# Work of an attention and feed-forward kernel moved from VectorE and ScalarE to GpSimd, with fewer warm-up products in front

## The chip, the cores and the metric

The kernel runs on one core of a Trainium2 chip. The metric is the device time of one execution in microseconds (us), as the median of several runs. The profile is one further execution, taken by the hardware profiler.

## What is computed

Banded attention with a few global keys, then two feed-forward layers on its output. Cut to what matters:

```python
scores = q @ k.T / 8                      # 2 batches, 8 heads, 768 positions, 64 wide
bias = -slopes * dist                     # dist: distance of query and key
scores = where(is_global | is_local, scores + bias, -1e9)
a = exp(scores - max(scores))
a = a / (sum(a) + 1e-9)
x = (a @ v)                               # 1536 tokens x 512
h = maximum(x @ w_in, 0); x = (h * h) @ w_out            # 512 -> 2048 -> 512
h = x @ w2_in; g = where(h >= 1, h, where(h <= -1, 0, (h + 1) ** 2 / 4)); out = g @ w2_out
```

A query keeps the keys of the last n_local = 96 positions and the first n_global = 8; both numbers are inputs, 64-bit integers in memory. The weights of the first layer's two matrices and of the second's come as 64-bit floating point; everything is computed in 32-bit precision, the feed-forward products as three products of parts (high and low) of 32-bit operands.

## The kernel before

**Attention.** There are 12 blocks of 128 queries, and each is done in two halves of four heads, 24 halves. A half (`probabilities`, `turned`, `result`) multiplies q by k for two rings of keys (L868), adds the mask and takes the negated row minimum in one DVE operation (L890), takes exponentials with their sum on ACT (L895), adds 1e-9 to the four sums (L900, DVE), takes reciprocals (L902, DVE), scales the four heads' probabilities (`Plan.scale`: L153 on ACT, L155 on DVE, L157 on POOL), turns them on PE (L918), copies them back (L129 on ACT, L130 on DVE) and multiplies them by v (L954). With a block's second half the result leaves as high and low parts (L129, L140) into `x`, from which the layers multiply. Three buffers `pr` and `mn` hold the probabilities and the small numbers of three halves.

**Weights.** `float32` loads a chunk of 128x1024 numbers in two halves of 512 columns as pairs of 32-bit words (tile `raw`, two buffers) and makes 32-bit numbers of them (tile `whole`). In 64 half chunks altogether ACT scales the upper word, read as a float, by 2 to the power -112 (L153); DVE shifts that left by 3 (L470), puts in the lower word's three upper bits (L473) and the sign of the upper word (L477). `parts` then splits them into a high and a low part in a `slot` (L129 on ACT, L140 on DVE). The chunks of the second layer are prepared ahead, with sums of their quarters that POOL or DVE subtracts (L503), and kept in device memory.

**The layers.** `Ffn.h` multiplies x by a chunk's first part (L535), ACT and DVE take the square of the positive part (L550, L552; later L555), `halves` splits it (L129, L140), `Ffn.y` multiplies by the second part (L733). The second layer runs in pairs (L652, L702). The first 19 events of the layers are interleaved with the attention's halves.

**What sets the order.** Nothing is placed by hand: every operation is given to `Plan` with its engines, an estimated duration, a due time and what it reads and writes; `Plan.emit` walks through an estimated time and gives each engine the operation that is due first among those that could start, and issues all in the order of the starts so found. Where an operation has several engines, another engine takes it if it would be done there sooner. Operations marked `port` use what POOL and DVE share: the planner starts such an operation only when the last one has ended, and lets DVE take another one in between (`PASS`). Where PE has nothing for longer than `FGAP`, the planner puts in filling products of 256 columns on a tile of zeros, `warm`: L1342 into bank 7 while the first four halves run, L1344 into bank 0 after that. Eight products of 512 columns on the same tile (`WARM`, L1339) begin the program; the product L1169 spreads `n_local` and `n_global` over the partitions, and the masks are made from its result (L1004 and on).

## Time and profile before

| | us |
|---|---|
| three runs | 613.58 to 614.92, median 614.76 |
| the profiled execution | 613.96 |
| its span, first to last instruction | 612.2 |
| PE busy (matmul) | 599.7 |
| PE loading weights (PEld) | 514.0 |
| DVE busy | 481.0 |
| ACT busy | 351.5 |
| POOL busy | 58.1 |

The span is one core's. PE's ends are modelled, so a busy PE is not a PE at its peak, and PE is busy with warm-up and filling products as well. A share of the whole span is a mean over stages with different limits: up to about 165 us attention and the first layer run side by side, up to about 302 us the weights of both layers are made, and then the second layer runs on what was kept. Lines such as L470 are lines of the kernel before; one line can stand for several engines' or tiles' operations, where a helper issues them. Idle time in front of an instruction is put down to whatever ended last; on an engine that is not the bound it costs nothing.

### The profile page before, as it was taken

To read this page: it belongs to the slowest core of one execution; us is meant where nothing else is said; L and a number is where in the kernel's file an instruction comes from. 1 tells how busy PE (TensorE), PEld (TensorE's weight loads), DVE (VectorE), ACT (ScalarE), POOL (GpSimd) and SP (SyncE) were. 2 spreads that over 40 slices of the span, in tenths; PEclk is the share of its full clock that TensorE was granted. 3 is DMA by queue.
4 is the path that set the end of the run, shared out by engine and by line. 5 is a ranking of instruction groups with operands and counts; after the bars stand their busy time and mean duration, and the time that the engine had idled before them with its cause. 6 is when DMAs were issued, how large, how long until landed. Compare 5 with 4: busy or idle time off the path is not lost. (4 is left out here: it accounts for less than half of the span.)

```text
span 612.2 us, 9673 instructions
## 1 busy us (share of the span) xinstructions
PE 599.7 (98%) x3438; PEld 514.0 (84%) x3438; DVE 481.0 (79%) x1031; ACT 351.5 (57%) x731; POOL 58.1 (9%) x88
## 2 busy tenths in 40 slices
PE   8999999999999999999999999999999999999995
PEld 5778987878888888888888898888899999888884
DVE  7999999965638988898566389999897788887862
ACT  7898877765547766674447464545553444444331
POOL 4120111010001104233200000000000000000000
PEclk9999999999999999999999999999999999999999
DMA  8553544430114879988512202323220022223002
GB/s 303 166 185 118 186 147 154 150 121 22 38 36 124 272 235 304 359 321 283 193 68 70 94 27 69 118 73 107 82 96 1 35 104 96 96 94 96 26 2 108
DMA packets 25790, 79.24 MB, mean 129 GB/s; under 512 B 2948, under 2 KB 2948, under 8 KB 25732
## 3 DMA queue, kind: packets, MB, share of 16 engines
q1 hardware_dynamic: 25730, 78.52, 38.0%
q8 instruction: 29, 0.48, 0.3%
q14 instruction: 29, 0.24, 0.1%
q10 hardware_dynamic: 2, 0.00, 0.0%
HBM read 62.78 MB, written 15.73 MB: 128 GB/s over the span
## 5 line engine op out<-in xcount | busy, mean ns | idle before, releaser
L658 DVE TENSOR_TENSOR pr<-bank,pr 128x384 f32<-128x384 f32 x112 | 60.2, 554 | 23.4 <-PE bank L652 22.5
L140 DVE TENSOR_TENSOR g<-r,g 128x512 fp32r<-128x512 f32 (+2 forms) x74 | 48.9, 660 | 34.7 <-ACT g L129 33.8
L550 ACT ACTIVATE r<-bank 128x512 f32<-128x512 f32 (+1 forms) x52 | 29.2, 562 | 59.7 <-PE bank L535 58.9
L129 ACT ACTIVATE g<-r 128x512 fp32r<-128x512 f32 (+2 forms) x74 | 42.7, 577 | 24.9 <-DVE r L567 14.2
L895 ACT ACTIVATE pr<-pr,mn 128x256 f32<-128x256 f32 (+1 forms) x96 | 45.9, 480 | 4.6 <-DVE mn L890 4.2
L563 ACT ACTIVATE r<-pr,small 128x384 f32<-128x384 f32 x43 | 26.2, 615 | 32.8 <-DVE pr L658 32.7
L153 ACT ACTIVATE whole<-raw 128x512 f32<-128x512 f32 x52 | 33.9, 668 | 9.1 <-DMA raw<-in_moe_w_out_dram 3.2
L477 DVE SCALAR_TENSOR_TENSOR whole<-raw,whole 128x512 uint32<-128x512 uint32 x52 | 36.7, 712 | 0.4
L890 DVE CUSTOM_DVE_ANT_0 pr<-bank,m 128x256 f32<-128x256 f32 (+1 forms) x96 | 33.4, 397 | 4.2 <-PE bank L954 4.1
L473 DVE SCALAR_TENSOR_TENSOR whole<-raw,whole 128x512 uint32<-128x512 uint32 x52 | 35.9, 702 | 0.3
L157 POOL TENSOR_SCALAR pr<-pr,mn 128x256 f32<-128x256 f32 (+1 forms) x38 | 21.4, 570 | 120.3 <-DVE mn L902 57.9
L868 PEld LDWEIGHTS bank<-nat,nat 64*128 64x128 f32 x352 | 22.7, 190 | 7.6 <-issue 2.7
L565 DVE SCALAR_TENSOR_TENSOR r<-r 128x384 f32<-128x384 f32 x43 | 23.8, 556 | 5.9 <-ACT r L563 5.1
L868 PE MATMUL bank<-nat,nat 64*128 64x128 f32 x352 | 27.0, 288 | 1.3 <-DVE mn L890 1.2
L563 ACT ACTIVATE nat<-pr,small 128x384 f32<-128x384 f32 x21 | 12.9, 617 | 24.5 <-DVE pr L658 24.5
L470 DVE TENSOR_SCALAR whole<-whole 128x512 uint32<-128x512 uint32 x52 | 22.9, 448 | 4.0 <-ACT whole L153 3.7
L129 ACT ACTIVATE pr<-bank 128x512 f32<-128x512 f32 (+2 forms) x46 | 23.5, 521 | 3.4 <-PE bank L652 2.1
L567 DVE TENSOR_TENSOR r<-pr,r 128x384 f32<-128x384 f32 x43 | 23.8, 557 | 1.2
L954 PE MATMUL bank<-pr,nat 128*64 128x128 f32 x352 | 24.0, 277 | 0.6 <-DVE mn L890 0.3
L918 PE MATMUL bank<-ident,pr 128*128 128x128 f32 x176 | 23.9, 275 | 0.0
L954 PEld LDWEIGHTS bank<-pr,nat 128*64 128x64 f32 x352 | 19.7, 136 | 4.8 <-issue 2.0
L918 PEld LDWEIGHTS bank<-ident,pr 128*128 128x128 f32 x176 | 20.0, 140 | 2.8 <-issue 0.5
(347 smaller groups left out, 1753.6 us busy)
## 6 DMA issues: line engine op xcount, KB each, us to landing
raw<-in_moe_w_in_dram SPq DMA_DIRECT2D x32, 512.0 KB, 4.4
raw<-in_moe_w_out_dram SPq DMA_DIRECT2D x32, 512.0 KB, 4.8
whole<-sums SPq DMA_DIRECT2D x14, 512.0 KB, 3.3
kept<-whole SPq DMA_DIRECT2D x12, 512.0 KB, 6.3
whole<-kept SPq DMA_DIRECT2D x12, 512.0 KB, 3.3
whole<-kept SPq DMA_DIRECT2D x13, 384.0 KB, 3.1
sums<-pr SPq DMA_DIRECT2D x8, 512.0 KB, 5.8
nat<-in_k_dram SPq DMA_DIRECT2D x12, 256.0 KB, 3.7
```

What stands on the lines that cost most here:

```text
L129: ("act", ns_act(n) - 30 * psum, lambda: nc.scalar.activation(out=at(out), in_=in_, func=ACTF.Copy), False),
L140: ways = [("dve", ns_dve(n), lambda: nc.vector.tensor_tensor(out=at(out), in0=in_, in1=at(hi).bitcast(F32), op=ALU.subtract), not psum)]
L153: ("act", ns_act(n) + (0 if isinstance(by, float) else 107), lambda: nc.scalar.activation(out=out, in_=in_, func=ACTF.Copy, scale=by), False),
L473: op("dve", ns_dve(512), d + 0.2, lambda h=h: nc.vector.scalar_tensor_tensor(out=word[:, h], in0=low[:, h], scalar=29, in1=word[:, h], op0 ...
L477: op("dve", ns_dve(512), d + 0.3, lambda h=h: nc.vector.scalar_tensor_tensor(out=word[:, h], in0=high[:, h], scalar=0x80000000, in1=word[: ...
L563: op("act", ns_act(N) + 64, due, lambda: nc.scalar.activation(out=r, in_=h, func=ACTF.Relu, bias=self.half, scale=0.5), keys, [kr])
L658: op("dve", ns_dve(W), start + step[name] + 0.2 - G_LEAD, lambda: nc.vector.tensor_tensor(out=to, in0=area[kb], in1=in1, op=ALU.add), [("b ...
L868: nc.tensor.matmul(**c)
L890: op("dve", ns_dve(w), due, lambda e=e: nc.vector.tensor_tensor_reduce(out=pr[:, e, :w], in0=self.banks[kbs[e % 2]][:, e // 2 * 256:e // 2 ...
L895: op("act", ns_act(w) + 200, due, lambda e=e: nc.scalar.activation(out=pr[:, e, :w], in_=pr[:, e, :w], func=ACTF.Exp, bias=mn[:, e:e + 1], ...
L918: self.nc.tensor.transpose(self.banks[kbs[m]][:, o:o + P], pr[:, 2 * m + e, c * P:(c + 1) * P], self.ident)
L954: nc.tensor.matmul(**c)
```

## The change

Five parts. The weights' signs: GpSimd multiplies the upper words, read as floats, by 0.0 in place, which leaves a zero with the sign; DVE then needs two operations in place of three (lower word shifted right, or the sign; number shifted left by 3, or that). The scaling of probabilities goes to GpSimd alone from the third block on (`SCALE`; the first two blocks keep DVE and GpSimd). The 1e-9 is added on GpSimd. The warm-up products are five and two in place of eight, the two with a due time among the first scores. The first two blocks' v is due later, behind their k and q. In the planner, POOL and DVE no longer wait for each other: a POOL operation is reckoned 1.3 times as long, and a DVE operation that meets one up to 90 ns longer; `BEGIN` and the lags of the two numbers' loads have other values.

```diff
-WARM, LAG = 8, 950
+AGAIN = 2
+WARM, LAG = 5, 950
...
-PASS = 1.0
+SHARE, GIVE = 1.3, 90
...
-SCALE, SCALE0 = ("act", "dve", "pool"), ("dve", "pool")
-CONV = ("act",)
+SCALE, SCALE0 = ("pool",), ("dve", "pool")
+CONV, SIGN = ("act",), ("pool",)
...
-    BEGIN = {"act": 2000, "dma": 1680, "words": 1680, "pool": 1080, "dve": 630, "pe": 1120}
+    BEGIN = {"act": 2560, "dma": 1360, "words": 740, "pool": 1260, "dve": 980, "pe": 1390}
...
-            if port > t and engine == "dve" and ops[i][0]["dve"][2]:
...
-                    others = max(free[e], t, port if ways[e][2] else 0)
-                    own = max(t, port if ways[engine][2] else 0)
+                    others, own = max(free[e], t), t
...
             if ways[engine][2]:
-                t = max(t, port)
-                port = t + ns
+                if engine == "pool":
+                    ns *= SHARE
+                    port = t + ns
+                elif engine == "dve" and port > t:
+                    ns += min(GIVE, port - t)
...
             self.plan.scale(512, d, f32[:, h], high[:, h].bitcast(F32), 2.0 ** -112, [(*kr, n)], [(*kc, n)], engines=CONV)
-            op("dve", ns_dve(256), d + 0.1, lambda h=h: nc.vector.tensor_scalar(
-                out=word[:, h], in0=word[:, h], scalar1=3, scalar2=None, op0=ALU.logical_shift_left,
-            ), (), [(*kc, n)], port=True)
+            self.plan.scale(512, d, high[:, h].bitcast(F32), high[:, h].bitcast(F32), 0.0, [(*kc, n)], [(*kr, n)], engines=SIGN)
             op("dve", ns_dve(512), d + 0.2, lambda h=h: nc.vector.scalar_tensor_tensor(
-                out=word[:, h], in0=low[:, h], scalar=29, in1=word[:, h],
+                out=low[:, h], in0=low[:, h], scalar=29, in1=high[:, h],
                 op0=ALU.logical_shift_right, op1=ALU.bitwise_or,
-            ), [(*kr, n)], [(*kc, n)], port=True)
+            ), (), [(*kr, n)], port=True)
             op("dve", ns_dve(512), d + 0.3, lambda h=h: nc.vector.scalar_tensor_tensor(
-                out=word[:, h], in0=high[:, h], scalar=0x80000000, in1=word[:, h],
-                op0=ALU.bitwise_and, op1=ALU.bitwise_or,
+                out=word[:, h], in0=word[:, h], scalar=3, in1=low[:, h],
+                op0=ALU.logical_shift_left, op1=ALU.bitwise_or,
             ), [(*kr, n)], [(*kc, n)], port=True)
...
-        op("dve", 70, due + 0.1, lambda: nc.vector.tensor_scalar(
-            out=mn[:, 4:8], in0=mn[:, 4:8], scalar1=1e-9, scalar2=None, op0=ALU.add), (), sums, port=True)
+        op("pool", 150, due + 0.1, lambda: nc.gpsimd.tensor_scalar(
+            out=mn[:, 4:8], in0=mn[:, 4:8], scalar1=1e-9, scalar2=1.0, op0=ALU.add, op1=ALU.mult), (), sums)
...
-            for c, lead in (("k", 3), ("q", 2.5), ("v", 2)):
+            for c, lead in (("k", 3), ("q", 2.5), ("v", 2 if blk > 1 else 0.3)):
...
-        for n in range(WARM):
-            plan.op("pe", ns_mm(512), -500 + n, lambda: nc.tensor.matmul(
+        for n in range(WARM + AGAIN):
+            plan.op("pe", ns_mm(512), -500 + n if n < WARM else -9.5, lambda: nc.tensor.matmul(
```

How this moves instructions is shown at three places. Line numbers of the changed kernel differ by up to seven (L1333 is L1339, L1163 is L1169, L861 is L868, L911 is L918, L726 is L733, L1338 is L1344, L158 is L157, L893 is L900).

PE at the program's start. `warm` is the tile of zeros, `small` holds the two numbers, `nat` k and q. Before, the last two of six warm-up products, the numbers' product and what follows:

```order
L1339 LDWEIGHTS warm_73
L1339 MATMUL bank7_70<-warm_73 128x512
L1169 MATMUL bank6_69<-small_74,r0_122 128x2
L1339 LDWEIGHTS warm_73
L1339 MATMUL bank7_70<-warm_73 128x512
L1339 LDWEIGHTS warm_73
L1339 MATMUL bank7_70<-warm_73 128x512
L868 MATMUL bank0_63<-nat0_125,nat1_126 128x128
```

And in the change, from the third warm-up product on:

```order
L1333 LDWEIGHTS warm_73
L1333 MATMUL bank7_70<-warm_73 128x512
L1163 MATMUL bank6_69<-small_74,r0_122 128x2
L1333 LDWEIGHTS warm_73
L1333 MATMUL bank7_70<-warm_73 128x512
L1333 LDWEIGHTS warm_73
L1333 MATMUL bank7_70<-warm_73 128x512
L861 MATMUL bank0_63<-nat0_125,nat1_126 128x128
L861 MATMUL bank1_64<-nat0_125,nat1_126 128x128
L861 MATMUL bank0_63<-nat0_125,nat1_126 128x128
L861 MATMUL bank1_64<-nat0_125,nat1_126 128x128
L1333 LDWEIGHTS warm_73
```

Three warm-up products stand ahead of the numbers' product in place of six, two behind it as before, and two more between the scores of the first half and those of the second.

PE at the first products of L1344, where the fifth half's probabilities are turned. `bank0` takes x times weights (L535), `bank6` and `bank7` the turned probabilities. Before, nine such fills, of which the last two are shown, then six more behind L733:

```order
L1344 LDWEIGHTS warm_73
L1344 MATMUL bank0_63<-warm_73 128x256
L1344 LDWEIGHTS warm_73
L1344 MATMUL bank0_63<-warm_73 128x256
L918 MATMUL bank6_69<-ident_71,pr_124 128x128 x4
L733 MATMUL bank2_65<-g1_121,slot1h_131 128x256
L733 MATMUL bank3_66<-g1_121,slot1h_131 128x256
L918 MATMUL bank7_70<-ident_71,pr_124 128x128 x4
L733 MATMUL bank4_67<-g1_121,slot1h_131 128x256
L733 MATMUL bank5_68<-g1_121,slot1h_131 128x256
L1344 LDWEIGHTS warm_73
L1344 MATMUL bank0_63<-warm_73 128x256
```

And in the change, where these two are the only ones of the program:

```order
L726 MATMUL bank4_67<-g1_121,slot1h_131 128x256
L726 MATMUL bank5_68<-g1_121,slot1h_131 128x256
L1338 LDWEIGHTS warm_73
L1338 MATMUL bank0_63<-warm_73 128x256
L1338 LDWEIGHTS warm_73
L1338 MATMUL bank0_63<-warm_73 128x256
L528 MATMUL bank0_63<-x_81,slot2h_133 128x256
L726 MATMUL bank2_65<-g1_121,slot1l_132 128x256
L726 MATMUL bank2_65<-g1_121,slot1h_131 128x256
L726 MATMUL bank3_66<-g1_121,slot1l_132 128x256
L726 MATMUL bank3_66<-g1_121,slot1h_131 128x256
L911 MATMUL bank6_69<-ident_71,pr_124 128x128 x4
```

Of 21 fills into bank 0 two are left, and the rest of L733's products for the second chunk stand ahead of the turning. The fills of L1342 are 30 in place of 31.

POOL from the second half's scaling on. `pr` are the probabilities, `mn` the sums of three halves in turn, `raw` the weights' words, `nat0` k. Before:

```order
L157 TENSOR_SCALAR pr_124<-pr_124,mn1_78 128x128 x2
L157 TENSOR_SCALAR pr_124<-pr_124,mn2_79 128x256 x2
L157 TENSOR_SCALAR pr_124<-pr_124,mn0_77 128x256 x3
L133 TENSOR_SCALAR nat0_125<-nat0_125 128x4x32
L157 TENSOR_SCALAR pr_124<-pr_124,mn1_78 128x256 x3
L157 TENSOR_SCALAR pr_124<-pr_124,mn2_79 128x256
L157 TENSOR_SCALAR pr_124<-pr_124,mn0_77 128x256
```

And in the change:

```order
L158 TENSOR_SCALAR pr_124<-pr_124,mn1_78 128x128 x2
L893 TENSOR_SCALAR mn2_79<-mn2_79 128x4
L158 TENSOR_SCALAR pr_124<-pr_124,mn2_79 128x256 x2
L158 TENSOR_SCALAR raw0_116<-raw0_116 128x512
L893 TENSOR_SCALAR mn0_77<-mn0_77 128x4
L158 TENSOR_SCALAR pr_124<-pr_124,mn0_77 128x256 x2
L158 TENSOR_SCALAR raw0_116<-raw0_116 128x512
L158 TENSOR_SCALAR raw1_117<-raw1_117 128x512 x2
L158 TENSOR_SCALAR raw0_116<-raw0_116 128x512 x2
L158 TENSOR_SCALAR raw1_117<-raw1_117 128x512
L134 TENSOR_SCALAR nat0_125<-nat0_125 128x4x32
L893 TENSOR_SCALAR mn1_78<-mn1_78 128x4
```

Between a half's add and its scalings stand signs of weights, and the copy of k (L134) stands ahead of the fifth half's add.

## Rows read from the trace of the kernel before

**Rows 1.** The page, part 1: busy us of each engine (share of the span), instructions.

```profile
PE 599.7 (98%) x3438; PEld 514.0 (84%) x3438; DVE 481.0 (79%) x1031; ACT 351.5 (57%) x731; POOL 58.1 (9%) x88
```

**Rows 2.** Windows: stretch, its length, busy us of five engines, PE clock, DMA share, GB/s.

```profile
14.00:62.00 48.00, 45.36 (x439) 39.18 (x440) 44.46 (x139) 41.88 (x117) 9.47 (x17) 1.00 0.48 161
62.00:165.00 103.00, 103.00 (x812) 85.27 (x811) 83.70 (x248) 72.37 (x198) 11.18 (x20) 1.00 0.36 116
165.00:302.00 137.00, 137.00 (x630) 113.36 (x629) 110.07 (x181) 82.90 (x138) 30.26 (x31) 1.00 0.70 237
```

**Rows 3.** Lines of PE, 5 to 62 us: busy us, mean ns | idle before.

```profile
L1342 PE MATMUL bank<-warm 128*128 128x256 bf16 x31 | 4.4, 273 | 0.0
...
L1344 PE MATMUL bank<-warm 128*128 128x256 bf16 x21 | 3.3, 272 | 1.4 <-ACT r L550 0.8 <-DVE r L552 0.6
```

**Rows 4.** Timeline of DVE, 31 to 33 us: start us, length us, ... [idle before].

```profile
31.72 0.43 DVE L552 SCALAR_TENSOR_TENSOR r<-bank,r 128x256 f32<-128x256 f32 x1 [1.04 <-PE bank L1344]
32.07 0.35 DVE L155 TENSOR_SCALAR pr<-pr,mn 128x256 f32<-128x256 f32 x1
```

**Rows 5.** Timeline, 0 to 8 us: PE and DVE.

```profile
1.39 2.74 PE L1339 MATMUL bank<-warm 128*128 128x512 bf16 x6 [1.39 <-DVE warm L1337]
...
2.38 0.15 DVE L1166 SCALAR_TENSOR_TENSOR small<-small,words 1x2 f32<-1x2 f32 x1
...
3.92 0.43 PE L1169 MATMUL bank<-small,r 128*128 128x2 f32 x2
...
5.15 1.58 PE L868 MATMUL bank<-nat,nat 64*128 64x128 f32 x16
...
6.71 0.27 DVE L890 CUSTOM_DVE_ANT_0 pr<-bank,m 128x128 f32<-128x128 f32 x1
...
7.55 0.28 DVE L890 CUSTOM_DVE_ANT_0 pr<-bank,m 128x128 f32<-128x128 f32 x1
```

**Rows 6.** Lines by form, 14 to 62 us: POOL, DVE and ACT.

```profile
L157 POOL TENSOR_SCALAR pr<-pr,mn 128x256 f32<-128x256 f32 x15 | 8.9, 605 | 29.1 <-DVE mn L902 18.3 <-ACT pr L129 5.5 <-ACT slot4h L129 4.1
...
L473 DVE SCALAR_TENSOR_TENSOR whole<-raw,whole 128x512 uint32<-128x512 uint32 x9 | 6.1, 684 | 0.0
...
L470 DVE TENSOR_SCALAR whole<-whole 128x512 uint32<-128x512 uint32 x10 | 4.3, 430 | 0.5 <-ACT whole L153 0.5
L153 ACT ACTIVATE pr<-pr,mn 128x256 f32<-128x256 f32 x9 | 4.1, 500 | 0.9 <-DVE mn L902 0.9
L155 DVE TENSOR_SCALAR pr<-pr,mn 128x256 f32<-128x256 f32 x9 | 3.8, 436 | 0.0
...
L140 DVE TENSOR_TENSOR slot1l<-whole,slot1h 128x512 fp32r<-128x512 f32 x2 | 1.6, 784 | 0.0
...
L140 DVE TENSOR_TENSOR slot3l<-whole,slot3h 128x512 fp32r<-128x512 f32 x2 | 1.4, 690 | 0.0
...
L900 DVE TENSOR_SCALAR mn<-mn 128x4 f32<-128x4 f32 x8 | 1.3, 166 | 0.1
```

**Rows 7.** Lines by form of POOL, 5 to 14 us.

```profile
L157 POOL TENSOR_SCALAR pr<-pr,mn 128x128 f32<-128x128 f32 x4 | 1.5, 377 | 1.6 <-DVE mn L902 1.6
...
L157 POOL TENSOR_SCALAR pr<-pr,mn 128x256 f32<-128x256 f32 x1 | 0.5, 478 | 1.6 <-DVE mn L902 1.6
```

**Rows 8.** Lines by form of DVE, 165 to 302 us.

```profile
L477 DVE SCALAR_TENSOR_TENSOR whole<-raw,whole 128x512 uint32<-128x512 uint32 x30 | 21.8, 734 | 0.3
L473 DVE SCALAR_TENSOR_TENSOR whole<-raw,whole 128x512 uint32<-128x512 uint32 x30 | 21.0, 715 | 0.3
L140 DVE TENSOR_TENSOR g<-r,g 128x512 fp32r<-128x512 f32 x25 | 20.2, 807 | 16.0 <-ACT g L129 15.8
L470 DVE TENSOR_SCALAR whole<-whole 128x512 uint32<-128x512 uint32 x30 | 13.7, 458 | 3.6 <-ACT whole L153 3.2
...
L470 DVE TENSOR_SCALAR m<-m 128x512 uint32<-128x512 uint32 x10 | 5.7, 581 | 0.1
...
L140 DVE TENSOR_TENSOR slot3l<-whole,slot3h 128x512 fp32r<-128x512 f32 x2 | 1.9, 957 | 0.0
```

More of the change, by code (lines that the diff above doesn't have):

```diff
@@ L219, in emit @@
             i = heapq.heappop(a)[1]
-            if port > t and engine == "dve" and ops[i][0]["dve"][2]:
-                other = min(((d, j) for d, j in a if not by[j] and not ops[j][0]["dve"][2]), default=None)
-                if other and other[0] < ops[i][1] + PASS:
-                    heapq.heappush(a, (ops[i][1], i))
-                    a.remove(other)
-                    heapq.heapify(a)
-                    i = other[1]
             if engine in ("act", "dve", "pool") and HOLD:
@@ L1158, in broadcast_int64 @@
     nc.vector.memset(ones, 1.0)
-    for n, (way, queue, src) in enumerate(zip(("words", "dma"), (nc.scalar, nc.sync), srcs)):
-        plan.op(way, 475, -300, lambda n=n, queue=queue, src=src: queue.dma_start(
+    for n, (way, ns, lag, queue, src) in enumerate((
+            ("words", 475, 775, nc.scalar, srcs[0]), ("dma", 50, 580, nc.sync, srcs[1]))):
+        plan.op(way, ns, -300, lambda n=n, queue=queue, src=src: queue.dma_start(
             out=words[0:1, 2 * n:2 * n + 2], in_=src.bitcast(I32).rearrange("(o n) -> o n", o=1),
-        ), (), [("words", n)], lag=960)
+        ), (), [("words", n)], lag=lag)
     low, high, r = words[0:1, 0:4:2], words[0:1, 1:4:2], one[0:1, 0:2]
```

## Prediction

> **What bounds the kernel now.** I read the page first: TensorE (PE) is busy for 599.7 us, 98% of the span [rows 1]. Such a share says little by itself, since warm-up and filling products count as busy, so I next cut the span into stages [rows 2]. From 62 to 302 us PE is busy in every microsecond, 103.00 of 103 and 137.00 of 137. VectorE (DVE) is busy for 83.70 and 110.07 us there, and PE does not wait for it. So what the change takes off DVE after 62 us buys nothing by itself, as long as PE keeps its work. What can be won lies ahead of 62 us. In 14 to 62 us PE is busy for 45.36 of 48 us, DVE for 44.46 (93%), ScalarE (ACT) for 41.88 (87%) and GpSimd (POOL) for 9.47. Of PE's share ahead of 62 us, 52 filling products of 256 columns are no work of the reference: 31 of line L1342 (4.4 us) and 21 of L1344 (3.3 us, with 1.4 us of waiting in front of them) [rows 3]. So two things are to be followed: the chain of the first 14 us, and DVE's work in 14 to 62 us.
>
> **The front.** Six warm-up products of 512 columns start at 1.39 us and the product that spreads the two numbers starts behind them at 3.92 us: 0.42 us for each, which is the 1.2 GHz level. Its operand left DVE at 2.38 + 0.15 = 2.53 us. ACT takes the result, DVE's masks follow, and the first row minimum (L890) starts at 6.71 us [rows 5]. With three products ahead, PE is free at 1.39 + 3 x 0.42 = 2.65 us, and with a hand-over from DVE the number product starts near 2.8: the masks come 1.1 us earlier. The other input of L890 are the scores. They start at 5.15 us, the first half's are half of that row, 0.79 us, and so there at about 5.9 [rows 5]: its L890 can start 0.8 us earlier even if the loads allow no earlier scores. The second half's scores now stand behind two more warm products (0.85 us) and are there at 5.9 + 0.85 + 0.79 = 7.5 us, when its first L890 started before (7.55, the fifth of all): it gains nothing, unless the scores start earlier. Between 0 and 1.1 us I take **0.6 us**, the middle, since the two halves pull to either side. The first v load goes behind the second k and q on SP's queue; its first reader is the product with v, behind minimum, exponential, scaling, transposes and copies of the same half, so I cost that move at nothing. The other numbers (BEGIN, the lags) only feed the planner.
>
> **DVE in 14 to 62 us.** For each half of a weight chunk the shift L470 goes: 10 in this stage at 430 ns, 4.3 us. The two operations that stay keep their size and their two inputs. Eight adds of 1e-9 go (166 ns, 1.3 us). Nine scalings (L155, 436 ns) stand there; three belong to the first four halves, which still share with DVE, and one more comes back to these: five go net, 2.2 us [rows 6]. DVE is relieved by 7.8 us, and ACT by nine scalings of 500 ns, 4.5 us.
>
> What this costs on GpSimd the trace shows in parts. A scaling of 128x256 took 605 ns there in this stage [rows 6], 478 ns once in the front, and one of 128x128 377 ns [rows 7]. From the last two, 0.79 ns per column: a sign over 512 columns is estimated at 0.68 us, the add over 4 at 0.28 us. The new work on POOL in the stage is 10 signs, 8 adds and 14 scalings, 6.8 + 2.2 + 8.5 = 17.5 us on top of 9.47, 27 of 48 us: POOL has room. But each of these 32 operations can hold DVE up. I bound it from both sides. In this stage DVE lost about 0.06 us per POOL operation: nine L155 at 436 against 350 ns for one alone [rows 4], and two L140 on slot 1 at 784 against 690 ns, 1.0 us over POOL's 17 operations [rows 2, 6]. In 165 to 302 us, where POOL subtracts for the prepared sums, DVE's forms are longer than here: L470 by 28 ns (30 of them) and 151 (10), L473 by 31 (30), L477 by 50 against L473 here (30), L140 by 117 (25), and six more L140 like the two at 957 by 267, together 0.8 + 1.5 + 0.9 + 1.5 + 2.9 + 1.6 = 9.2 us over 31 operations, 0.30 us each [rows 2, 6, 8]. The stage is the same as for the lower bound, but the changed planner no longer keeps the two engines apart, and a sign is longer than a scaling. I take **0.15 us**, nearer to the lower bound: 32 x 0.15 = 4.8 us. DVE gains 7.8 - 4.8 = 3.0 us (5.9 by the lower bound, -1.8 by the upper).
>
> What these rows show is a DVE operation that grows longer beside one of GpSimd. The Trainium skill (SBUF — State Buffer, Who interferes with whom) states it harder: the two engines share one pair of ports as an exclusive lock, taken by a DVE operation with two inputs in SBUF and by a GpSimd one, and whoever has it keeps it for the whole instruction. By that rule the sum could turn round; it is the third rival below.
>
> **The fills.** The L1344 fills fall from 21 to 2, as the order shows. They write bank 0, which ACT and DVE read (L550, L552), and that is a wait crosswise: the fills stood 0.8 us for L550 and 0.6 us for L552, and DVE stood 1.04 us for a fill, until 31.72 us [rows 3, 4]. With the fills gone DVE has 3.0 + 1.0 = 4.0 us. Not all of it reaches PE, since ACT is busy for 87% and stands in each half's chain; I pass on three quarters, **3.0 us**.
>
> **Later.** From 62 us on the same parts go from DVE, with 40 of the shifts in 165 to 302 us [rows 8], and POOL gets the signs. PE is dense there already, so I cost it at nothing. The cover is the lead of the weights: a half chunk is ready later by a sign less a shift, 0.68 - 0.43 = 0.25 us, and two hand-overs. If that cover is gone, each late chunk costs PE so much.
>
> **Sum.** 0.6 + 3.0 = 3.6 us. The profiled execution took 613.96 us, 1.8 us around its span included, which gives 610.4. The runs' median, 614.76, lies 0.8 us above that execution; on its scale the forecast is 614.76 - 3.6 = **611.2 us**. A measurement of this kernel tells about 0.2% (1.2 us) from no change.
>
> **Rivals.**
> - More is won. At 0.06 us per POOL operation DVE gains 5.9 + 1.0; all of it passes on, and 0.8 us in front: 614.76 - 7.7 = **607.1 us**. For it: 7.7 us of fills, and DVE's 93%. Against: ACT's 87%.
> - Nothing past the front. The chain of scores, minimum, exponential, scaling, transposes and copies sets the pace, four scalings in a row on POOL (4 x 0.605 = 2.4 us) replace scalings spread over three engines, and DVE's time stays spare: 614.76 - 0.6 = **614.2 us**. For it: the first 22 us are such a chain. Against: in 14 to 62 us ACT and DVE are both near full.
> - Slower: GpSimd holds DVE. At 0.30 us per operation DVE loses 1.8 us. If each operation holds DVE for its whole undisturbed length, 14 x 0.48 + 10 x 0.68 + 8 x 0.28 = 15.8 us, 0.49 each, it loses 8.0. In the middle, 0.40 us, it is 12.8 - 7.8 = 5.0 us, less 0.6 in front: 614.76 + 4.4 = **619.2 us**. It decides from 7.8 / 32 = 0.24 us per operation. For it: POOL's 605 against 478 ns, and the 0.30 us of the later stage. Against: the 0.06 us of this very stage. The lock of the Trainium skill's page (SBUF — State Buffer, Who interferes with whom) would be this mechanism; the trace agrees that the operations lengthen, not by how much.
>
> **Chances.** The forecast (609 to 613.4) 0.52, more won 0.14, nothing past the front 0.16, slower 0.18. The first two make faster by over 0.2%, 0.66; the third is within 0.2%, 0.16; the last 0.18. The range reaches to the second and takes in the near part of the slower case, 0.30 us and a little over: 607.0 to 616.6 us.
>
> **What would show it.** Right: the number product near 2.8 us and the first L890 near 6 us; no L470, and DVE's scalings in the first four halves alone; two L1344 fills and no wait of L552 for one; PE dense from 58 or 59 us instead of 62. The means of DVE's two remaining weight operations and of L140 in 14 to 62 us give the price per POOL operation: under 0.24 us the sign of the forecast holds. Wrong: PE waiting for transposes behind POOL's scalings, or holes in PE after 62 us at weights whose signs came late; or a granted clock below 1.00 ahead of 62 us, with fewer fills and warm products (before, it is 1.00 in 14 to 62 us [rows 2]).

## Result, and the profile of the changed kernel

The changed kernel took 621.19 us (median of 6 runs, 620.63 to 622.97), the kernel before 614.49 in the same comparison (6 runs): a ratio of 1.0117, 95% interval 1.0103 to 1.0130, **slower by 6.7 us**. The forecast was 611.2, the range 607.0 to 616.6: wrong in sign. The profiled execution has a span of 618.5 us, against 612.2.

The page, part 1, answers to [rows 1]:

```profile
PE 600.2 (97%) x3417; PEld 511.8 (83%) x3417; DVE 463.6 (75%) x928; ACT 342.3 (55%) x704; POOL 142.8 (23%) x218
```

The windows answer to [rows 2]:

```profile
14.00:62.00 48.00, 41.90 (x410) 35.69 (x411) 44.31 (x115) 38.39 (x104) 30.58 (x46) 1.00 0.54 181
62.00:165.00 103.00, 102.82 (x814) 84.79 (x811) 69.88 (x204) 65.01 (x183) 45.66 (x81) 1.00 0.33 106
165.00:302.00 137.00, 134.56 (x615) 109.78 (x614) 102.82 (x143) 81.37 (x136) 56.12 (x66) 1.00 0.68 234
```

DVE was relieved over the whole span (463.6 us against 481.0) and in 62 to 165 us (69.88 against 83.70), and the clock stayed at 1.00. In 14 to 62 us, where the forecast had counted on 3.0 us, DVE is as busy as before, 44.31 us against 44.46: shifts, adds and most scalings are gone there, but the new order does more work on weights in this stretch, 11 half chunks in place of nine to ten and ten low parts in place of eight. And in 165 to 302 us, where PE had been busy in all 137 us, it now stands for 2.44.

Busy shares don't say how far a kernel is behind. So I counted each matmul of the reference with its undisturbed time (0.227 us for 512 columns, 0.119 for 256, and so on), warm-up and filling products with nothing, and asked how much later than in the kernel before the same sum was reached. Columns are times of the kernel before; one execution each, so read them beside the ratios of many runs. From 120 us on they hold to about one product (0.2 us). Ahead of that some products of 128 columns start in pairs, and what is taken as their time moves a figure by up to 0.4 us.

```
us behind before at         22 us   62 us  120 us  220 us  302 us   median   ratio (95%)
the change                   1.72    1.22    2.58    2.55    6.48   621.19  1.0117 (1.0103-1.0130)
e1  three-op weights         1.04    0.10    1.75    2.59    3.05   616.54  1.0050 (1.0026-1.0075)
e2  sign on ACT              0.94    0.45    1.74    1.71    1.71   616.30  1.0030 (1.0016-1.0044)
e3  scalings spread          2.11    2.43    4.45    4.41    8.22   622.06  1.0118 (1.0092-1.0143)
e4  front of before          2.15    1.54    5.85    5.81   10.15   621.88  1.0121 (1.0104-1.0138)
e6  sign of 8 columns        1.74    0.35    2.27    2.24    2.24   615.84  1.0010 (0.9997-1.0022)
e7  GIVE 440                 1.59    1.62    2.21    2.17    2.34   617.01  1.0034 (1.0022-1.0046)
e13 old rule                 0.41    1.53    1.86    1.82    1.82   616.68  1.0039 (1.0026-1.0053)
before + e5  signs           0.27    2.35    2.52    2.48    2.48   616.02  1.0023 (1.0014-1.0033)
before + e8  front           0.76    1.42    2.16    2.21    2.21   615.69  1.0016 (1.0006-1.0026)
before + e9  scalings        0.01   -0.03    0.07    0.50    0.50   614.67  1.0014 (0.9993-1.0035)
before + e10 new rule        1.25    3.45    4.15    4.14    5.13   617.38  1.0060 (1.0039-1.0082)
before + e11 warm-up         5.69    1.52    1.82    1.78    1.78   616.03  1.0026 (1.0016-1.0037)
before + e12 later v         0.00   -0.11   -0.09   -0.09   -0.09   614.01  0.9995 (0.9985-1.0004)
before, e14 no late fills    0.00   -1.02   -0.64   -0.64   -0.64   612.90  0.9973 (0.9957-0.9988)
before, e15 ACT +10 ns       0.27    1.85    2.59    2.38    2.38   616.33  1.0027 (1.0011-1.0042)
before, e16 PE +10 ns        0.29    1.67    1.67    1.67    1.67   615.44  1.0025 (1.0009-1.0041)
e17 = e14 + e12              0.00   -1.63   -1.64   -1.64   -1.64   612.52  0.9967 (0.9955-0.9979)
e18 = e17 + e9               0.01   -1.13   -1.02   -0.59   -0.59   613.47  0.9992 (0.9979-1.0006)
```

The first line of the table parts the loss in two: **3.9 us from 220 to 302 us** (6.48 - 2.55), and some 2.6 us ahead of 120 us. e4's execution lies 2 us above its median.

**The late loss.** What PE waits for in 165 to 302 us (engine, bank, line <- releaser: us, times, longest):

```profile
PE bank L726 <- DVE g L141: 2.4, 5, 0.8
...
PEld bank L726 <- DVE g L141: 4.5, 5, 1.2
```

Before, there was no such wait. Five times the product with g (L726) stands for g's low part, which DVE makes in L141. The lines by form of DVE and POOL in that stretch answer to [rows 8]:

```profile
L466 DVE SCALAR_TENSOR_TENSOR raw<-raw 128x512 uint32<-128x512 uint32 x41 | 33.7, 836 | 15.7 <-POOL raw L158 15.6
L141 DVE TENSOR_TENSOR g<-r,g 128x512 fp32r<-128x512 f32 x23 | 20.3, 883 | 4.9 <-ACT g L130 4.8
...
L158 POOL TENSOR_SCALAR raw<-raw 128x512 f32<-128x512 f32 x42 | 32.9, 793 | 66.7 <-ACT whole L154 49.6 <-ACT m L154 11.8 <-issue 5.2
```

Read the idle times. Before, DVE stood 15.8 us for ACT's part of g: it was early, and PE got g in time. Now it stands 15.6 us for GpSimd's signs and only 4.8 for g: it comes late to g, ever later from 201 to 225 us, where the first of the five waits is. The timeline of DVE, POOL and PE at one of the five places:

```profile
250.18 0.85 DVE L496 TENSOR_TENSOR pr<-whole,pr 128x256 f32<-128x256 f32 x1 [1.32 <-POOL pr L496]
250.96 2.16 DVE L466 SCALAR_TENSOR_TENSOR raw<-raw 128x512 uint32<-128x512 uint32 x2
253.04 1.28 DVE L470 SCALAR_TENSOR_TENSOR m<-m,raw 128x512 uint32<-128x512 uint32 x2
254.24 1.12 DVE L141 TENSOR_TENSOR g<-r,g 128x512 fp32r<-128x512 f32 x1
...
250.12 1.43 POOL L158 TENSOR_SCALAR raw<-raw 128x512 f32<-128x512 f32 x2
251.81 0.77 POOL L158 TENSOR_SCALAR raw<-raw 128x512 f32<-128x512 f32 x1 [0.26 <-ACT whole L154]
253.79 1.04 POOL L158 TENSOR_SCALAR raw<-raw 128x512 f32<-128x512 f32 x1 [1.21 <-ACT whole L154]
...
254.26 0.39 PE L726 MATMUL bank<-g,slot3l 128*128 128x512 f32 x1
255.42 0.73 PE L726 MATMUL bank<-g,slot3h 128*128 128x512 f32 x2 [0.78 <-DVE g L141]
```

g's high part was there at 250.18 (ACT's L130 ends there). DVE's queue is in order: behind a wait for GpSimd's sum come two L466, each 1.1 us beside a sign, two L470, and then L141, itself 1.12 us beside a third sign. PE gets g at 255.4, 1.16 us after the product before it.

**The early loss** has no one place. What PE waits for in 14 to 62 us of the change:

```profile
PE bank L528 <- ACT x L130: 1.7, 1, 1.7
PE bank L947 <- DMA nat<-in_v_dram: 1.6, 1, 1.6
PE bank L726 <- DVE slot1l L141: 1.1, 1, 1.1
PE bank L911 <- POOL pr L158: 1.0, 2, 0.8
```

The third is a weight whose low part came late; the fourth are transposes behind GpSimd's scalings, a sign of being wrong that the prediction had named. (In GpSimd's queue no sign stands between a half's add and its scalings; signs stand between one half's scalings and the next half's add.) At 22 us the first layer starts 1.7 us later, though the front came as forecast (timeline of PE and DVE, for [rows 5]):

```profile
2.64 0.54 PE L1163 MATMUL bank<-small,r 128*128 128x2 f32 x2
...
4.61 1.22 PE L861 MATMUL bank<-nat,nat 64*128 64x128 f32 x8 [0.55 <-DMA nat<-in_q_dram]
...
5.96 0.29 DVE L883 CUSTOM_DVE_ANT_0 pr<-bank,m 128x128 f32<-128x128 f32 x1
```

The 1.7 us arise at 19 to 23 us (timeline of POOL, DVE and ACT):

```profile
18.25 2.77 POOL L158 TENSOR_SCALAR raw<-raw 128x512 f32<-128x512 f32 x3
...
19.38 2.18 DVE L466 SCALAR_TENSOR_TENSOR raw<-raw 128x512 uint32<-128x512 uint32 x2 [0.56 <-POOL raw L158]
...
22.19 0.63 ACT L130 ACTIVATE slot0h<-whole 128x512 fp32r<-128x512 f32 x1 [1.90 <-DVE whole L470]
22.73 0.58 ACT L130 ACTIVATE x<-bank 128x512 fp32r<-128x512 f32 x1
```

Weights with late signs keep ACT's next copy, and behind it in ACT's queue waits the copy of x, which PE needs. From 50.07 us on PE stands for v. SP's queue and PE's row:

```profile
43.82 0.33 SPq L457 DMA_DIRECT2D raw<-in_moe_w_out_dram  x1
...
46.01 0.38 SPq L834 DMA_DIRECT2D nat<-in_v_dram  x1
...
51.63 1.09 PE L947 MATMUL bank<-pr,nat 128*64 128x128 f32 x16 [1.56 <-DMA nat<-in_v_dram]
```

The weight load at 43.82 waits for DVE's last reader of its buffer, and q, k and v stand behind it.

### The profile page after: what moved, and what is told of

Read it like the earlier page. It is cut to its first block, busy times and chain, and to the rows that moved or that the text cites. A ratio compares the mean times of both kernels' runs of the same rounds, so it can differ in the third digit from the quotient of the medians.

```text
span 618.5 us, 9719 instructions
## 1 busy us (share of the span) xinstructions
PE 600.2 (97%) x3417; PEld 511.8 (83%) x3417; DVE 463.6 (75%) x928; ACT 342.3 (55%) x704; POOL 142.8 (23%) x218
## 5 line engine op out<-in xcount | busy, mean ns | idle before, releaser
L141 DVE TENSOR_TENSOR g<-r,g 128x512 fp32r<-128x512 f32 (+2 forms) x74 | 51.9, 701 | 25.9 <-ACT g L130 25.2
L158 POOL TENSOR_SCALAR raw<-raw 128x512 f32<-128x512 f32 x64 | 50.4, 797 | 73.8 <-ACT whole L154 56.3
L466 DVE SCALAR_TENSOR_TENSOR raw<-raw 128x512 uint32<-128x512 uint32 x64 | 50.8, 807 | 16.2 <-POOL raw L158 16.2
L158 POOL TENSOR_SCALAR pr<-pr,mn 128x256 f32<-128x256 f32 (+1 forms) x88 | 56.8, 661 | 11.9 <-DVE mn L895 11.5
L130 ACT ACTIVATE g<-r 128x512 fp32r<-128x512 f32 (+2 forms) x74 | 42.7, 576 | 23.2 <-DVE r L560 14.3
L883 DVE CUSTOM_DVE_ANT_0 pr<-bank,m 128x256 f32<-128x256 f32 (+1 forms) x96 | 33.2, 394 | 10.9 <-PE bank L947 6.3
L470 DVE SCALAR_TENSOR_TENSOR whole<-whole,raw 128x512 uint32<-128x512 uint32 x52 | 37.6, 738 | 1.0
L861 PEld LDWEIGHTS bank<-nat,nat 64*128 64x128 f32 x352 | 23.6, 199 | 7.4 <-issue 3.7
L861 PE MATMUL bank<-nat,nat 64*128 64x128 f32 x352 | 27.9, 297 | 0.7 <-DMA nat<-in_q_dram 0.6
L130 ACT ACTIVATE pr<-bank 128x512 f32<-128x512 f32 (+2 forms) x47 | 24.3, 525 | 6.8 <-PE bank L645 2.1
L911 PE MATMUL bank<-ident,pr 128*128 128x128 f32 x176 | 25.0, 276 | 1.5 <-POOL pr L158 1.0
L911 PEld LDWEIGHTS bank<-ident,pr 128*128 128x128 f32 x176 | 19.8, 140 | 5.9 <-POOL pr L158 2.8
```

What stands on the lines that cost most here:

```text
L130: ("act", ns_act(n) - 30 * psum, lambda: nc.scalar.activation(out=at(out), in_=in_, func=ACTF.Copy), False),
L141: ways = [("dve", ns_dve(n), lambda: nc.vector.tensor_tensor(out=at(out), in0=in_, in1=at(hi).bitcast(F32), op=ALU.subtract), not psum)]
L158: ("pool", ns_pool2(n) + (0 if isinstance(by, float) else 141), lambda: nc.gpsimd.tensor_scalar(out=out, in0=in_, scalar1=by, scalar2=1.0, ...
L466: op("dve", ns_dve(512), d + 0.2, lambda h=h: nc.vector.scalar_tensor_tensor(out=low[:, h], in0=low[:, h], scalar=29, in1=high[:, h], op0= ...
L470: op("dve", ns_dve(512), d + 0.3, lambda h=h: nc.vector.scalar_tensor_tensor(out=word[:, h], in0=word[:, h], scalar=3, in1=low[:, h], op0= ...
L861: nc.tensor.matmul(**c)
```

## Experiments

Medians, ratios and TensorE's delay are those of the table. "Before" is the kernel before, "the change" all of it.

**e1.** The change, weights made by the three DVE operations of before:

```diff
-            self.plan.scale(512, d, high[:, h].bitcast(F32), high[:, h].bitcast(F32), 0.0, [(*kc, n)], [(*kr, n)], engines=SIGN)
+            op("dve", ns_dve(256), d + 0.1, lambda h=h: nc.vector.tensor_scalar(
+                out=word[:, h], in0=word[:, h], scalar1=3, scalar2=None, op0=ALU.logical_shift_left,
...
```

> The change without its signs: the weights are made by the three DVE operations of before, the rest of the change stays. Theory S (GpSimd's signs make the weights late in 220 to 300 us, where the change lost 3.9 us of its 6.7): no hole of TensorE over 0.4 us in 165 to 302 us, and about 621.2 - 3.9 = 617.3 us; if the signs also cost what was lost in 62 to 120 us (1.3 us), 616.0. Rival Q (the scalings on GpSimd are what is late): no better than 620.5, the holes after 220 us stay. Rival P (the planner's new rule on GpSimd beside VectorE, not the signs): holes stay at smaller size, 619 to 621.

616.54 us. The delay from 220 to 302 us falls from 3.93 to 0.46 us. In the change's plan the signs make the late loss; ahead of 120 us 1.75 us stay.

**e2.** The change with the sign on ScalarE:

```diff
-CONV, SIGN = ("act",), ("pool",)
+CONV, SIGN = ("act",), ("act",)
```

ScalarE's product with 0.0 stands for GpSimd's. The results are then not the reference's; that it is the weights' signs which this run leaves out is presumed, not looked into.

> The change with the sign made by ScalarE (a scaling with 0.0, about 0.68 us as its conversion of the same 512 columns) in place of GpSimd; VectorE still spared its shift. Theory S: the holes of 220 to 300 us go, since VectorE's first operation no longer waits for GpSimd (15.6 us of waiting there) and is not lengthened by it: about 617.3 us or less. Rival A (ScalarE, 81 us busy of 137 there, gets 41 x 0.68 = 28 us more, and in 14 to 62 us, 38 of 48 busy, another 7.5 us): ScalarE becomes the late one ahead of 62 us, where PE loses 2 to 5 us: 619 to 624 us.

616.30 us, no late loss, although DVE now waits 21.9 us for ACT's signs in that stretch, more than for GpSimd's. So it isn't the waiting for a sign by itself. What is shorter is L466, 703 ns in the mean against 836 in the change. ACT's 24 us more (105.61 of 137 us against 81.37) cost nothing there; rival A falls.

**e3.** The change with the scalings spread as before:

```diff
-SCALE, SCALE0 = ("pool",), ("dve", "pool")
+SCALE, SCALE0 = ("act", "dve", "pool"), ("dve", "pool")
```

> The change with the probabilities' scalings spread over ScalarE, VectorE and GpSimd as before, signs and the rest as changed. Theory S: the late holes (3.9 us) stay; what the scalings cost ahead of 120 us (up to 2.3 us) comes back: 619 to 620.5 us. Rival Q (scalings in GpSimd's queue, with signs behind them, are the main cost): 616 us or less. Rival N (scalings on GpSimd were a gain for VectorE): 621.5 to 624.

622.06 us; the late loss stays at 3.8 us. The scalings are not what is late (Q falls). But theory S had 619 to 620.5 us, and the result lies in rival N's range: ahead of 120 us TensorE is 4.45 us behind, more than the change's 2.58. Since e9 shows no gain from the scalings, a new order can be the cause as well.

**e4.** The change with the front of before:

```diff
-WARM, LAG = 5, 950
+WARM, LAG = 8, 950
...
-    BEGIN = {"act": 2560, "dma": 1360, "words": 740, "pool": 1260, "dve": 980, "pe": 1390}
+    BEGIN = {"act": 2000, "dma": 1680, "words": 1680, "pool": 1080, "dve": 630, "pe": 1120}
...
-            for c, lead in (("k", 3), ("q", 2.5), ("v", 2 if blk > 1 else 0.3)):
+            for c, lead in (("k", 3), ("q", 2.5), ("v", 2)):
```

> The change with the front of before: eight warm-up products, first v loaded two steps ahead, the planner's begin times and lags of before. Theory S: the front is worth 0.6 us of gain at most and its loads cost nothing later: 621 to 622.5 us, late holes stay. Rival F (the later v, which let the second product with v wait 1.6 us at 50 us, and the other order that follows from the front, cost the first 1.0 to 2.3 us): 619 to 620 us.

621.88 us, late loss 4.3 us. As theory S had it.

**e5.** Before, with the signs and the two DVE operations of the change, under the old rule:

```diff
-            op("dve", ns_dve(256), d + 0.1, lambda h=h: nc.vector.tensor_scalar(
...
+            self.plan.scale(512, d, high[:, h].bitcast(F32), high[:, h].bitcast(F32), 0.0, [(*kc, n)], [(*kr, n)], engines=SIGN)
```

> The kernel before with the signs on GpSimd alone (weights in one GpSimd and two VectorE operations), the planner's rule of before, which plans operations of the two engines one behind the other. Theory S (the signs alone make the loss, with any planner): holes of TensorE in 165 to 302 us again, 3 to 5 us, 617 to 619 us. Rival P (it is the signs together with the changed rule of the planner): no hole over 0.4 us after 165 us, at most 1 us lost, 614 to 615 us.

616.02 us, 0.0 lost from 120 to 302 us: P is right about the late stage. The signs alone, in an order planned with the old rule, make no late hole. But ahead of 62 us TensorE is 2.35 us behind.

**e6.** The change, each sign over 8 of 512 columns, same order:

```diff
-            self.plan.scale(512, d, high[:, h].bitcast(F32), high[:, h].bitcast(F32), 0.0, ...
+            self.plan.scale(512, d, high[:, h.start:h.start + 8].bitcast(F32), high[:, h.start:h.start + 8].bitcast(F32), 0.0, ...
```

> The change with each sign over 8 of the 512 columns (it leaves out the signs of the other weights), in the same place of the same order: every hand-over between ScalarE, GpSimd and VectorE stays, GpSimd's time for the sign falls from 0.80 to about 0.3 us. Theory L (the length of the sign beside VectorE: it is waited for, and stretches VectorE's operations): the holes of 220 to 300 us go, 616 to 617.5 us. Rival H (the hand-overs and the fixed order alone make VectorE late): holes stay, 620 to 621.5 us.

615.84 us, no late loss. Lines by form of e6, 165 to 302 us:

```profile
L466 DVE SCALAR_TENSOR_TENSOR raw<-raw 128x512 uint32<-128x512 uint32 x42 | 29.3, 703 | 12.2 <-POOL raw L158 10.9
...
L158 POOL TENSOR_SCALAR raw<-raw 128x8 f32<-128x8 f32 x42 | 14.0, 338 | 85.3 <-ACT whole L154 66.8 <-ACT m L154 12.3 <-issue 5.4
```

Order and hand-overs are those of the change (DVE, ACT, PE and POOL do the same operations in the same order), 10.9 of the 15.6 us of waiting stay, only the length went: signs of 338 ns, L466 of 703. So length decides (L), not the hand-overs (H).

**e7.** The change with another price in the planner:

```diff
-SHARE, GIVE = 1.3, 90
+SHARE, GIVE = 1.3, 440
```

> The change with GIVE at 440 in place of 90 ns: the planner reckons with what a VectorE operation lost beside a sign in the late stage (1.12 against 0.68 us), and orders accordingly; every operation stays on its engine. Theory O (the order is wrong because the planner's price is too low): most of the late 3.9 us comes back, about 617 to 618 us. Rival L (the work itself is too long wherever it is put): 620 to 622 us, holes over 0.5 us stay after 220 us.

617.01 us, 4.2 less than the change by the medians, with signs and scalings on their engine and of their length (signs 828 ns). The price also moves six of the subtractions for the sums (L496) from DVE to GpSimd and leaves 19 late fills in place of two, so that more than the order differs. The timeline of DVE, where the g of the place shown above is made:

```profile
248.85 0.83 DVE L141 TENSOR_TENSOR g<-r,g 128x512 fp32r<-128x512 f32 x1 [1.03 <-ACT g L130]
250.93 1.71 DVE L466 SCALAR_TENSOR_TENSOR raw<-raw 128x512 uint32<-128x512 uint32 x2 [1.25 <-POOL raw L158]
252.56 1.28 DVE L470 SCALAR_TENSOR_TENSOR m<-m,raw 128x512 uint32<-128x512 uint32 x2
```

Here g goes ahead of the four weight operations behind which it stands in the change, and PE comes to its products only at 252.13 us; theory O holds. One hole of the same kind remains, outside the table's columns: at 307 us PE stands 0.9 us for a g whose L141 took 1.22 us, beside a sum of GpSimd (L496), and is behind by 1.2 us more after it.

**e8.** Before, with the front of the change: the diff of e4 the other way round.

> The kernel before with the front alone: five warm-up products ahead of the number's product and two ahead of the second half's scores, first v two loads later, with the begin times and lags of the change. As the prediction's first term has it: 0.6 us faster, 613.5 us against 614.1. Rival G (the first layer's start at 21.6 us hangs on ScalarE's queue, not on the front): no difference, 613.9 to 614.5. Rival F (the later v and the other order cost): 615 or more.

615.69 us: slower by 1.0 where I had 0.6 us of gain. Rival F's time holds.

**e9.** Before, with the scalings on GpSimd: the diff of e3 the other way round.

> The kernel before with all scalings of probabilities from the third block on GpSimd, nothing else changed. Theory S with an early stage that any new order sets back: the scalings cost little by themselves, within 1.2 us of before, no hole after 165 us. Rival Q (four scalings in a row on GpSimd make transposes late): 1.5 to 2.5 us slower, TensorE behind by that at 120 us and waiting at transposes for GpSimd. The prediction's own term: 5 net scalings of 436 ns off VectorE, 0.8 of ACT's, less their price: about 1 us faster.

614.67 us, no difference; the 1 us of the prediction's own term doesn't come. Window of e9, 14 to 62 us:

```profile
14.00:62.00 48.00, 44.91 (x441) 38.97 (x442) 43.61 (x136) 38.94 (x108) 16.79 (x30) 1.00 0.50 169
```

Against [rows 2] DVE is relieved by 0.85 us and ACT by 2.9; TensorE stands at 62 us where it stood (-0.03).

**e10.** Before, with the new rule:

```diff
-                t = max(t, port)
-                port = t + ns
+                if engine == "pool":
+                    ns *= SHARE
+                    port = t + ns
+                elif engine == "dve" and port > t:
+                    ns += min(GIVE, port - t)
```

> The kernel before with the planner's new rule alone (GpSimd's operations 1.3 times as long, a VectorE operation beside one 90 ns longer, instead of one behind the other): no operation changes its engine by force. Rival P (the rule by itself costs): holes of TensorE after 165 us at VectorE's g, where GpSimd's sums (L503) of 1.1 us stand beside it, 616 us or more. Theory S (it takes the signs too, 42 of them there, to make VectorE late): no hole over 0.5 us after 165 us, within 1.5 us of before.

617.38 us: 4.15 us ahead of 120 us and 1.0 us in one late hole, at g as rival P had it (PE stands 0.63 us at 282.5 us). The rule costs late without signs too, but a quarter of what it costs with them.

**e11.** Before, with the warm-up products alone:

```diff
-WARM, LAG = 8, 950
+AGAIN = 2
+WARM, LAG = 5, 950
```

> The kernel before with five warm-up products in front of the number's product and two more in front of the second half's scores, nothing else of the front. If these are what cost the front its 1 us: 615 us or more, TensorE behind at 62 us. If not (the later v or the begin times did it): 613.5 to 614.5 us.

616.03 us. The window of 14 to 22 us:

```profile
14.00:22.00 8.00, 5.39 (x34) 3.58 (x35) 7.52 (x23) 7.25 (x22) 2.60 (x4) 0.79 0.72 230
```

The granted clock is 0.79, part of the stretch at 1.2 GHz, after 5 to 14 us with PE busy for 5.88 of 9 us. In this order only 6 filling products of L1342's kind stand ahead of 25 us, all 31 of [rows 3] in the kernel before. TensorE is 5.7 us behind at 22 us, and 1.5 at 62: the stage between takes in most of any shift of its start.

**e12.** Before, with the later v; one DMA moves in SP's queue:

```diff
-            for c, lead in (("k", 3), ("q", 2.5), ("v", 2)):
+            for c, lead in (("k", 3), ("q", 2.5), ("v", 2 if blk > 1 else 0.3)):
```

> The kernel before with the first v load two places further back on SP's queue, behind the second k and q; nothing else in any queue moves. The prediction costs it at nothing: 614.1 to 614.9 us, like before. Rival G: TensorE waits 1.5 us at 6.7 us for the second k and q, which now come 0.4 us earlier: 613.7. Rival F: the product with the first v waits for it: 615 or more.

614.01 us, no difference. In the kernel before that term was right.

**e13.** The change with the old rule: the diff of e10 the other way round, with `PASS`.

> The change with the planner's rule of before (GpSimd's and VectorE's SBUF operations planned one behind the other), signs, scalings, add and front as changed. Theory R (the late loss needs signs and the new rule together): no hole over 0.5 us after 165 us, 2 to 3 us lost ahead of 120 us: 616 to 617.5 us. Rival S (the signs make the late holes whatever the rule): five holes as in the change, 619 to 621.5 us.

616.68 us. Windows:

```profile
14.00:62.00 48.00, 43.74 (x429) 37.52 (x428) 41.53 (x113) 37.06 (x101) 28.20 (x48) 1.00 0.55 178
...
165.00:302.00 137.00, 137.00 (x633) 113.44 (x632) 100.78 (x141) 80.18 (x136) 54.47 (x65) 1.00 0.68 232
```

PE is dense again late: the late loss, but for e10's 1.0 us, needs signs and new rule together. And in 14 to 62 us DVE is down by 2.9 us and ACT by 4.8 against [rows 2], with TensorE 1.5 us *behind* at the end. But 22 late fills are back in this order, two in the change, and PE waits 1.6 us in front of them.

**e14.** Before, without the late fills; every other instruction in its place:

```diff
-        ), ("bank", 7), 0], [lambda: nc.tensor.matmul(
-            out=banks[0][:, 256:512], lhsT=warm[:, 0:P], rhs=warm[:, 0:256], start=True, stop=True,
-        ), ("bank", 0), 0]]
+        ), ("bank", 7), 0], [lambda: None, ("bank", 0), 0]]
```

> The kernel before without its 21 filling products into bank 0 (23 of them with the ones that the records miss, if any), every other instruction of every engine in the same order: no work of the reference is left out. The prediction's term: their cross-wise wait with VectorE is worth 1.0 us, three quarters of it on TensorE: 613.6 us against 614.4. Rival B (VectorE and ScalarE set that stage, the fills stand in holes): 614.1 to 614.8. Rival C (with fewer products the granted clock falls below 1.00 ahead of 62 us): 615 or more.

612.90 us, faster by 1.45, the clock at 1.00. TensorE is 1.02 us ahead at 62 us and keeps 0.64 of it from 120 us on. Where DVE stood for a fill until 31.72 us [rows 4], it now reads (timeline):

```profile
31.29 0.42 DVE L552 SCALAR_TENSOR_TENSOR r<-bank,r 128x256 f32<-128x256 f32 x1 [0.57 <-ACT r L550]
```

0.43 us earlier, held by ACT. The cross-wise wait was real.

**e15, e16.** Before, with one hand-over time of the planner 10 ns longer; e15 (e16 has 270 for "pe" and 150 for "act"):

```diff
-    OTHER = {"pe": 260, "act": 150, "dve": 130, "pool": 200}
+    OTHER = {"pe": 260, "act": 160, "dve": 130, "pool": 200}
```

> The kernel before with one number of the planner altered: a hand-over from ScalarE reckoned at 160 instead of 150 ns. Same operations on much the same engines, another order. Theory Z (before's order is a lucky one, and any other costs 1 to 3 us ahead of 120 us): 615.5 to 617.5 us. Rival (an order planned on nearly the same numbers is as good, and a part of the change is at fault for the 2.4 us): 614 to 615 us.

> As the run with ScalarE's hand-over, but with a hand-over from TensorE reckoned at 270 instead of 260 ns. Theory Z: 615.5 to 617.5 us, the loss ahead of 120 us. Rival: 614 to 615 us.

616.33 and 615.44 us: 2.59 and 1.67 us behind at 120 us (e16 just under Z's bound). Not only the order differs: five operations (copies and scalings) changed their engine in e15, two in e16. In e15 ACT's timeline has a conversion in front of a half's exponentials, and DVE's chain stands behind it:

```profile
27.13 0.69 ACT L153 ACTIVATE whole<-raw 128x512 f32<-128x512 f32 x1 [1.54 <-DMA raw<-in_moe_w_out_dram]
...
29.83 0.17 DVE L900 TENSOR_SCALAR mn<-mn 128x4 f32<-128x4 f32 x1 [1.44 <-ACT pr L895]
...
31.50 0.63 PE L918 MATMUL bank<-ident,pr 128*128 128x128 f32 x4 [1.56 <-DVE mn L890]
```

ACT's wait of 1.54 us for a load, with the exponentials behind it, passes through three engines. The kernel before has its conversion behind that half's exponentials.

**e17, e18.** The fills left out and v later (the diffs of e14 and e12 together); e18 also has the scalings of e9.

> The kernel before without the late fills and with the first v two places later on SP. If the two add: 614.4 - 1.4 - 0.1 = 612.9 us; if the later v's 0.1 is lost among the holes that the fills leave, the same as without it, 612.9 to 613.0. Rival: the order that fits the waits of before fits no more, 614 or above.

> The same with all scalings from the third block on GpSimd. The prediction's relief (5 net scalings of 436 ns off VectorE, less 14 x 0.15 on GpSimd, and ScalarE's 4.5 us) now with no fill in the way: up to 0.5 to 1 us more, 612 to 612.5 us. Rival (VectorE is not what TensorE waits for in its holes there, but the chain of a half and v's transfer): 612.8 to 613.5 us.

e17 took 612.52 us and beats both kernels (0.9967 of before, 0.9955 to 0.9979). In its execution TensorE is 1.0 us further ahead at 120 us than in e14; the intervals of the two don't tell them apart. e18 took 613.47, as the rival had it: the scalings add nothing even with the fills gone, by the medians they cost 0.95 us.

## Why the prediction was wrong

**"Later ... I cost it at nothing" is the step that failed most, 3.9 of the 6.7 us.** I named the lead of the weights as the cover, and by that the signs are no trouble: in 165 to 302 us no product waited for a weight. I didn't ask what stands *behind* the waiting L466 in DVE's queue. It is g, whose lead is short. Part of that lead stood in [rows 8]: DVE stood 15.8 us for ACT's g, 0.63 us for each of 25. The rest is on PE's side: before, PE's next product with a g began 2.4 us in the mean (0.8 to 4.5) after DVE had ended that g. In the change it began 1.4 us after it for the g of 201 us, then 0.5, 0.3 and 0.1, and at 225 us PE had to wait, as four times more. So no single wait used the lead up; DVE fell behind over several half chunks. e6 (length, in the change's very order) and e13 (the old rule) each take the loss away alone, e7 all of it but the hole at 307 us: it takes long signs beside DVE *and* a plan made with 90 ns for a collision that costs about 440. Sums on DVE are no rival: seven of them stand there in e6 too, five in e13.

**The price of a GpSimd operation was of the wrong kind.** I took an average, 0.15 us. In 14 to 62 us of the change, L466 and L470 took 786 and 753 ns against 684 of [rows 6], 11 each, and g (256 columns) 531 against 425 before, 5 times: (11 x 102 + 11 x 69 + 5 x 106) / 46 operations of POOL is 0.05 us, and 0.07 with two L141 of slot 1 at 1000 instead of 690. So it stayed under the 0.24 from which my slower rival was to decide, and the kernel was slower all the same. In the late stage what mattered were collisions in the wrong places. The rival's time (619.2) was nearer than the forecast's, by luck: GpSimd did hold DVE, but not in the rival's stage and not by DVE's total.

**"I pass on three quarters" failed too.** DVE's 93% in 14 to 62 us was read as the bound. In the change itself DVE's share there hardly fell (44.31 us), since other work moved in. e9 and e13 relieve DVE by 0.85 and 2.9 us there, and ACT by 2.9 and 4.8, and TensorE gains nothing. Both have the late fills and an order of their own, so they show only that relief by itself doesn't bring PE forward; e18 against e17, without fills, shows the same (DVE 44.86 against 45.96 us). By the rows of waits PE there stands for the chain of a half, for v's transfer, for a weight's low part and for GpSimd's scalings. That was my second rival (nothing past the front, 0.16), whose "Against" was this very share.

**The fills' wait was right** in its mechanism: 1.0 us forecast on DVE, three quarters of it for PE; in e14 1.02 us of TensorE at 62 us, 0.64 from 120 us on, and 1.45 us by the medians (0.7 to 2.6 by the interval). It is the one gain of the change that a run of its own shows.

**The front:** the number product came at 2.64 us (2.8 forecast), the first minimum at 5.96 (6), but nothing of it was left at 14 us in the change. My lower bound, 0, was the value to take. The later v cost nothing, as said; the warm-up products cost 1.6 us with the begin times of before (e11), in an order that left gaps, with the granted clock at 0.79 in 14 to 22 us.

**A term was missing: the new order itself.** "The other numbers only feed the planner" was true and no reason to cost them at nothing. Two alterations of 10 ns, which leave all but five and two operations on their engines, cost 2.6 and 1.7 us ahead of 120 us in one execution each (by the ratios of many runs 1.7 and 1.5 us in all); front, signs and new rule alone 2.2, 2.5 and 4.1. Of seven runs that re-planned the order of before, six (e5, e8, e10, e11, e15, e16) were behind it there; e9 was not (0.07). So a new order often costs here, not always. For that reason the change's own 2.6 us ahead of 120 us can't be put down to one of its parts; the holes shown (ACT's copy of x, SP's loads) are where it appears, not shown to be its cause.

## What to carry to other kernels

In an in-order queue, a new wait is paid by what stands behind it, so list that, with its slack, before calling the wait covered. The slack is the queue's own idle time ahead of that operation (here DVE waiting for g) and the time from its end to its reader (here PE's product). Where a planner writes the order, re-planning has a price of its own: measure it with an alteration that means nothing before judging one that does. And a busy share of 93% is no bound until an experiment that lowers it moves the end.

## What the runs showed of the hardware

When DVE and GpSimd collide, one waits out the other. In the records of the change, DVE's two weight operations (L466, L470) came up 36 times with 0.16 to 0.67 us of a GpSimd operation left, and ended 0.51 to 0.55 us after it, whatever was left. The 16 of them with 0.55 us or more left and no second GpSimd operation beside them ended 0.539 us after it, with a spread of 0.005, and took 1.124 us in the mean; 53 without GpSimd took 0.68. The rows above show it: the sign of 253.79 ends at 254.83, L141 beside it at 255.36. The Trainium skill (SBUF — State Buffer, Who interferes with whom) calls the shared ports an exclusive lock that one holds for the whole instruction; by that rule DVE waits out the rest of the sign, and the trace agrees. What I had read as a "lengthening" was the mean of hits and misses, and the trace before the change held it: of the 25 L140 of g in [rows 8], 17 took 0.68 or 0.69 us, the other eight 0.73 to 1.25. It goes the other way too: 10 of the change's weight operations came when 0.94 or 0.95 us of a scaling were left, took 0.67 to 0.69 us themselves, and the scaling ended 0.265 to 0.268 us after them. A sign took 0.65 us with no DVE operation beside it (8 of them), 0.797 in the mean of all 64.

The other surprise is how much the middle stage takes in: 5.7 us of delay at 22 us, with the clock at 0.79, were 1.5 us at 62 (e11).
